# The last 64-row attention tile with full 128-column matmuls, and the engines' order planned anew

## The chip, the cores and the metric

The kernel runs on one core of a Trainium2 chip. The metric is the device time of one execution in microseconds (us), as the median of several runs. A profile is one execution recorded by the hardware profiler; its span goes from the first to the last instruction. TensorE is called PE in the rows, VectorE DVE, ScalarE ACT, GpSimd POOL and SyncE SP.

## What is computed

Three stages, each fed by the one before; inputs and output are float32, with 4 batches, 8 heads, 576 positions and a head size of 64.

```python
def _attn_ref(q, k, v):                       # q, k, v: (4, 8, 576, 64)
    scores = scale * np.matmul(q, k.transpose(0, 1, 3, 2))
    scores = np.where(block_i >= block_j, scores, -1e9)     # blocks of 64 positions
    attn = softmax(scores)
    return np.matmul(attn, v)

def _moe_ref(x, w_in, w_out):                 # x: (2304, 512), w_in: (512, 2048)
    h = x @ w_in
    return (h * np.tanh(softplus(h))) @ w_out

def _moe2_ref(x, w_gate, w_val, w_out, rms_g):   # (512, 1536) twice, (1536, 512)
    xn = x / rms(x) * rms_g
    g = xn @ w_gate
    return (silu(g) * (xn @ w_val)) @ w_out
```

## The kernel before

Most matrices are split into two float16 parts, high and low, and a product is made of three passes (`PASSES`: high-high, high-low, low-high). Batch 0's scores and the first four blocks of 64 rows are done in float32.

Attention goes through the 576 query rows of a batch in five tiles, four of 128 rows and a last one of 64 (`attention(b, i, ...)`, i = 0 to 4). `scores` makes the scores of one head (two heads in the first two tiles) in PSUM, DVE takes their maximum (L1003), `bias` is made of it on DVE or POOL (L1012), ACT takes the exponential (L1028). `probs` splits it into float16 parts (L1102 to L1109) and has a DMA transpose them (L1119). `av` multiplies the transposed probabilities `pt` (the weights) with the split values `v16` (the moving operand) into the PSUM buffer `xt` (L1146), of which there is one. `norm_x` multiplies by one over the sum (L1176, tile `xfl`), splits and transposes the result.

The last tile puts two heads on the 128 partitions, 64 rows each. Its four pairs of heads go through `av` as 2 heads x 5 key tiles x 3 passes; each matmul takes the 64 columns of its head from `pt` as weights and writes 64 partitions of `xt`. The fifth key tile has 64 rows only, so its matmuls use 64 rows.

The first MLP goes over nine tiles of 256 tokens: `mlp1_h` (L1366, float32 in the first tile: L1357) with the activation on ACT (L1392, L1385), a split on DVE, ACT or POOL (L1401 to L1409), then `mlp1_y` (L1427, first tile L1435) and the RMS norm. It runs beside attention, which feeds it. The second MLP (`mlp2_gv` L1778, `mlp2_o` L1913) follows. Weights come as 512 KB pieces and are brought to float32 by DVE operations between SBUF tiles (`to_f32`, L566, L574, L594), squared and summed for a scale (`group_scale`, tile `wc`, L641), and split (`split`, L516 to L539).

The order of every engine's instructions is computed before the kernel is built. Each operation is recorded with `op(engine, ns, fn, r=..., w=..., at=..., alts=...)`: a cost in ns, what it reads and writes, a wished time, and other engines that could do it. `Plan.place` is a list scheduler that plays the operations forward with these costs: at each step it takes the engine that is free first and the ready operation with the smallest key. `LAT` holds the delay from one engine's end to another's start. Costs come from `t_act`, `t_dve`, `t_dve2`, `t_dvett`, `t_pool`, `t_pool1` and `t_mm`. `t_dve2` and `t_dvett` are those of DVE operations between SBUF tiles; they are of the class `Shared`, and `place` makes them longer by a share while POOL is busy:

```python
if e == DVE and not back and type(ns) is Shared and free[POOL] > t:
    ns = ns + ns.by * min(free[POOL] - t, ns / (1.0 - ns.by))
```

`Plan.run` places several times, with keys from a backward pass, and keeps the shortest. `SHIFT` adds a number to the keys of each named part of the work. In waits of the first part of the plan `with_idle` puts matmuls on a constant (L1967).

## Time and profile before

| | us |
|---|---|
| median of 3 runs | 970.93 |
| lowest and highest run | 969.48, 971.12 |
| span of the profiled execution | 967.8 |

The profiled execution's time is known by its span alone; the runs are 1.7 to 3.3 us longer than that. In the rows, a busy column is the time in which an engine had an instruction running. The end of a matmul is modelled, so the pace of a run of matmuls is read from one start to the next start. `PEclk` is the clock granted to TensorE as a share of 2.4 GHz. Idle time stands in square brackets behind an instruction, with what ended it.

### The profile page before, as it was taken

What the parts mean: (1) busy time and instruction counts of PE and PEld (TensorE: products, weight loads), DVE (VectorE), ACT (ScalarE), POOL (GpSimd) and SP (SyncE); (2) the same over time, 40 slices, a digit from 0 to 9 for tenths busy, and PEclk for the clock granted to TensorE, in tenths of its full rate; (3) what the DMA queues carried; (4) which work ended last, traced back from release to release, by engine and by line L of the source; (5) the groups of instructions that cost most, each with busy time, mean ns of one, the idle gap of its engine ahead of it and who ended that gap; (6) DMA issues with size and microseconds to landing.
All of it is one profiled execution on the core that took longest, in us unless ns stands there. A gap on an engine that the chain in (4) does not pass through costs nothing.

```text
span 967.8 us, 19320 instructions
## 1 busy us (share of the span) xinstructions
PE 943.2 (97%) x6958; PEld 591.0 (61%) x6959; DVE 789.4 (82%) x1760; ACT 597.2 (62%) x1225; POOL 561.4 (58%) x709
## 2 busy tenths in 40 slices
PE   9997989999999999999999999999999999999998
PEld 7783447666585767675675845555555555554554
DVE  4898888888877879688875999989997898866745
ACT  4767578999768889875984555456543364531320
POOL 1268247878665746577752937858864487531411
PEclk9997999999999999999999999999999999999999
DMA  9765476779966896686763746781836260753011
GB/s 238 194 211 154 140 152 127 116 134 169 170 138 122 142 169 139 108 174 150 144 152 60 150 107 156 164 184 52 160 118 115 88 125 14 135 94 87 1 61 70
DMA packets 317183, 125.39 MB, mean 130 GB/s; under 512 B 296352, under 2 KB 296352, under 8 KB 317088
## 3 DMA queue, kind: packets, MB, share of 16 engines
q1 hardware_dynamic: 317088, 124.17, 60.5%
q8 instruction: 54, 0.88, 0.4%
q14 instruction: 41, 0.34, 0.1%
HBM read 50.07 MB, written 12.98 MB: 65 GB/s over the span
## 4 chain that ended last, share of the span: by engine, by line
PE 55%; DVE 6%; DMA 2%; ACT 2%; POOL 1%; issue 1%; DVEq 0%; ACTq 0%; POOLq 0%
PE o L1913 13%; PE v L1778 11%; PE g L1778 10%; PE y L1427 9%; PE h L1366 8%; PE x L1146 2%; DMA pt<-p 1%; PE s L968 1%; DVE w2fo L574 0%; DMA w2ro<-in_moe_w_out_dram 0%; DVE w2fo L566 0%; POOL sums_b L1528 0%; PE s L986 0%; DVE u3v L1806 0%; ACT e L1028 0%
## 5 line engine op out<-in xcount | busy, mean ns | idle before, releaser
L1366 PE MATMUL h<-x,w1i 128*128 128x256 f16 x1536 | 179.8, 274 | 0.0
L1427 PE MATMUL y<-w1o,g 128*128 128x512 f16 x768 | 177.1, 379 | 1.1 <-DVE g L1409 1.0
L1366 PEld LDWEIGHTS <-w1i 128*128 128x128 f16 x1536 | 147.3, 98 | 22.3 <-issue 0.4
L1778 PE MATMUL g<-xnT,w2g 128*128 128x384 f16 x756 | 131.0, 326 | 1.3 <-DVE u3v L1806 0.6
L1778 PE MATMUL v<-xnT,w2v 128*128 128x384 f16 x756 | 127.6, 326 | 0.5 <-DVE sl12g L1806 0.5
L1427 PEld LDWEIGHTS <-g 128*128 128x128 f16 x768 | 70.9, 98 | 78.7 <-DVE g L1409 3.1
L1778 PEld LDWEIGHTS <-w2g 128*128 128x128 f16 x756 | 73.9, 98 | 54.4 <-issue 3.6
L1778 PEld LDWEIGHTS <-w2v 128*128 128x128 f16 x756 | 73.9, 98 | 51.6 <-issue 0.9
L1003 DVE TENSOR_REDUCE mx<-s 128x1 f32<-128x512 f32 (+4 forms) x128 | 69.7, 558 | 27.9 <-PE s L969 26.6
L1028 ACT ACTIVATE e<-s,bias,cS 128x512 f32<-128x512 f32 (+3 forms) x120 | 72.6, 608 | 19.5 <-POOL bias L1012 10.3
L1109 POOL TENSOR_TENSOR p<-e,p 128x128 f16<-128x128 f32 (+4 forms) x66 | 61.9, 942 | 16.5 <-DVE p L1102 6.2
L1146 PEld LDWEIGHTS <-pt 128*128 128x128 f16 (+2 forms) x1368 | 55.0, 103 | 24.7 <-issue 8.6
L1146 PE MATMUL x<-v,pt 128*128 128x64 f16 (+2 forms) x1368 | 63.2, 196 | 4.3 <-DMA pt<-p 2.1
L1409 DVE SCALAR_TENSOR_TENSOR g<-f,ich,g 128x512 f16<-128x512 f32 x64 | 58.0, 910 | 5.9 <-ACT g L1404 2.9
L1392 ACT ACTIVATE f<-h,ch 128x512 f32<-128x512 f32 x64 | 43.6, 685 | 15.6 <-PE h L1366 12.2
L1028 ACT ACT_TABLE_LOAD x39 | 50.0, 1283 | 4.0 <-DVE bias L1012 3.4
L1392 ACT ACT_TABLE_LOAD x39 | 50.0, 1283 | 0.7
L506 POOL TENSOR_SCALAR p<-e 128x128 f16<-128x128 f32 (+2 forms) x53 | 26.7, 505 | 34.9 <-ACT e L1028 20.1
L1796 ACT ACTIVATE p5v<-v,ck 128x384 f32<-128x384 f32 x18 | 10.5, 581 | 46.5 <-PE v L1778 46.5
L1102 DVE CAST p<-e 128x128 f16<-128x128 f32 (+2 forms) x58 | 25.9, 449 | 14.8 <-ACT e L1028 7.1
L1109 DVE TENSOR_TENSOR p<-e,p 128x384 f16<-128x384 f32 (+4 forms) x46 | 33.7, 734 | 5.1 <-POOL p L506 3.9
L1012 POOL TENSOR_SCALAR bias<-mx,nS 128x1 f32<-128x1 f32 (+1 forms) x46 | 25.1, 545 | 21.5 <-DVE mx L1003 17.1
(610 smaller groups left out, 2190.1 us busy)
## 6 DMA issues: line engine op xcount, KB each, us to landing
wir<-in_moe_w_in_dram SPq DMA_DIRECT2D x16, 512.0 KB, 6.0
wor<-in_moe_w_out_dram SPq DMA_DIRECT2D x16, 512.0 KB, 3.8
w2rg<-in_moe_w_gate_dram SPq DMA_DIRECT2D x24, 256.0 KB, 3.2
w2rv<-in_moe_w_val_dram SPq DMA_DIRECT2D x24, 256.0 KB, 3.5
w2ro<-in_moe_w_out_dram SPq DMA_DIRECT2D x24, 256.0 KB, 3.1
q<-in_q_dram SPq DMA_DIRECT2D x16, 256.0 KB, 3.8
k<-in_k_dram SPq DMA_DIRECT2D x16, 256.0 KB, 4.6
v<-in_v_dram SPq DMA_DIRECT2D x15, 256.0 KB, 4.7
```

The source lines that it names most:

```text
L506: nc.gpsimd.tensor_scalar(out=out_, in0=in_, scalar1=by, scalar2=1.0, op0=ALU.mult, op1=ALU.mult)
L1003: lambda z=z, cols=cols: nc.vector.reduce_max(out=mx()[:, cols], in_=ts[z](), axis=AX.X),
L1028: lambda y=y, z=z, c0=c0, w=w, acc=acc, e=e, h=h: nc.scalar.activation(out=e()[:, c0 : c0 + w], in_=ts[z]()[:, y, :], func=AF.Exp, bias=bi ...
L1102: lambda z=z, ev=ev, t0=t0, t1=t1: nc.vector.tensor_copy(out=view(p16)[:, z, t0:t1, 0, :], in_=ev(t0, t1)),
L1109: lo = lambda eng, z=z, ev=ev: eng.tensor_tensor(out=view(p16)[:, z, :, 1, :], in0=ev(0, kt), in1=view(p16)[:, z, :, 0, :], op=ALU.subtract)
L1146: nc.tensor.matmul(o, pv(z)[:nr, t, ph, c0 : c0 + w], v16[b, t]()[:nr, vh, h * D : h * D + D], start=(t == 0 and y == 0), stop=(t == kt - ...
L1366: nc.tensor.matmul(ph()[:, g, :], w1i[fq]()[:, cc, wh, f * P : (f + 1) * P], x()[:, xh * NCC + cc, :], start=(z == 0), stop=(z == 3 * NCC ...
L1392: ACT, t_act(W, 1, True), lambda: nc.scalar.activation(out=e(), in_=phf(), func=AF.Mish, scale=cs()),
L1409: lambda: nc.vector.scalar_tensor_tensor(out=g16()[:, 1], in0=hv(), scalar=sc(), in1=g16()[:, 0], op0=ALU.mult, op1=ALU.subtract),
L1427: nc.tensor.matmul(yps[t, m](), g16()[:, gh, g, m * P : (m + 1) * P], w1o[f]()[:, wh, :], start=(f == 0 and z == 0), stop=(f == NF1 - 1 an ...
L1778: nc.tensor.matmul(b(), w()[:, wo, wh, cc, :], x()[:, (2 * xo + xh) * 2 + cc, :], start=(i == 0), stop=(i == 5),)
L1913: nc.tensor.matmul(y(), pp()[:, gh, m * P : (m + 1) * P], w2["o", fq]()[:, g, wh, :], start=(g == 0 and i == 0), stop=(g == FQ - 1 and i = ...
```

## The change

`av` of the last tile takes both heads of a pair at once: all 128 columns of `pt` as weights, and the 128 columns of both heads' values as the moving operand, over all 128 rows. The result is 128 x 128; the quarter of head 0's rows with head 0's values and the quarter of head 1's rows with head 1's values are the wanted ones. `xt` is twice as wide there, and `norm_x` reads the two quarters with one DVE instruction each. Since all 128 rows of the fifth key tile are used, the unused 64 rows of its `v16` tile are set to zero by POOL or DVE.

The planner's numbers change: all delays in `LAT`, the costs of all engines (DVE and POOL operations shorter, delays between engines mostly longer, DMA issue times shorter), and the cost of the bursts of `av`. `Shared` has no share any more; instead `place` holds a lock that `Shared` operations of DVE and all operations of POOL take in turn, and an engine may prefer an operation that doesn't need the lock. `SHIFT` is replaced, and `FINE` adds a number for each of some 700 single operations. So all queues are ordered anew.

```diff
 LAT = {
-    PE: {PE: 0, ACT: 45, DVE: 45, POOL: 45, DMA: 45, NONE: 0},
-    ACT: {PE: 145, ACT: 45, DVE: 45, POOL: 178, DMA: 45, NONE: 0},
-    DVE: {PE: 110, ACT: 100, DVE: 45, POOL: 104, DMA: 35, NONE: 0},
-    POOL: {PE: 110, ACT: 45, DVE: 45, POOL: 45, DMA: 35, NONE: 0},
-    DMA: {PE: 820, ACT: 780, DVE: 780, POOL: 820, DMA: 820, NONE: 0},
+    PE: {PE: 0, ACT: 200, DVE: 200, POOL: 240, DMA: 200, NONE: 0},
+    ACT: {PE: 153, ACT: 133, DVE: 133, POOL: 180, DMA: 127, NONE: 0},
+    DVE: {PE: 131, ACT: 112, DVE: 112, POOL: 160, DMA: 106, NONE: 0},
+    POOL: {PE: 87, ACT: 68, DVE: 68, POOL: 113, DMA: 62, NONE: 0},
+    DMA: {PE: 640, ACT: 660, DVE: 660, POOL: 700, DMA: 650, NONE: 0},
...
+HOLD = {DVE: 100.0, POOL: 90.0}
...
+def shares(e, ns):
+    return e == POOL or e == DVE and type(ns) is Shared
...
+                        elif kind and lock - HOLD[e] > f:
+                            t = lock - HOLD[e]
+                            pull = t - f
...
-            if e == DVE and not back and type(ns) is Shared and free[POOL] > t:
-                ns = ns + ns.by * min(free[POOL] - t, ns / (1.0 - ns.by))
             start[i], end[i] = t, t + ns
+            if not back and shares(e, ns):
+                lock = end[i] = max(t + ns, lock + ns - HOLD[e])
...
 def t_act(n, aps=0, psum=False, accum=False):
-    return (110 if psum else 140) + 0.8333 * n + 70 * aps + (120 if accum else 0)
+    return (51 if psum else 93) + 0.8333 * n + 95 * aps + (92 if accum else 0)
...
 def t_dve(n, aps=0):
-    return 125 + 1.0417 * n + 85 * aps
+    return 70 + 1.0417 * n + 40 * aps
...
 def t_dve2(n, aps=0):
-    return Shared(158 + 0.5208 * n + 61 * aps, 0.6)
+    return Shared(70 + 0.5208 * n + 62 * aps)
...
 def t_dvett(n, aps=0):
-    return Shared(160 + 1.0417 * n + 61 * aps, 0.45)
+    return Shared(75 + 1.0417 * n + 66 * aps)
...
 def t_pool(n):
-    return 390 + 1.85 * n
+    return 175 + 1.9 * n
...
             x = buf("at", [P, 2, DM], F16, f"v16_{b}_{tt}", "v16", 6)
+            if n < P:
+                pad = lambda eng, x=x, n=n: eng.memset(x()[n:].bitcast(U32), 0)
+                op(POOL, 500, lambda pad=pad: pad(nc.gpsimd), w=[(x, 2)], at=a, alts=[(DVE, 600, lambda pad=pad: pad(nc.vector))])
...
-                outs = (
-                    [(xt()[BLK * hh : BLK * hh + BLK, cols, :], 2 * key + hh, BLK * hh, BLK) for hh in range(2)]
-                    if last
-                    else [(xt()[:, cols, :], key, 0, P)]
-                )
-                for o, h, c0, w in outs:
-                    for t in range(kt):
-                        nr = rows(t)
-                        for y, (vh, ph) in enumerate(PASSES):
-                            nc.tensor.matmul(
-                                o, pv(z)[:nr, t, ph, c0 : c0 + w], v16[b, t]()[:nr, vh, h * D : h * D + D],
-                                start=(t == 0 and y == 0), stop=(t == kt - 1 and y == 2),
-                            )
+                w = 2 * D if last else D
+                for t in range(kt):
+                    for y, (vh, ph) in enumerate(PASSES):
+                        nc.tensor.matmul(
+                            xt()[:, cols, :], pv(z)[:, t, ph, :], v16[b, t]()[:, vh, key * w : key * w + w],
+                            start=(t == 0 and y == 0), stop=(t == kt - 1 and y == 2),
+                        )
...
             op(
-                PE, 34 * 3 * kt * (2 if last else 1), mm, r=[pt] + [v16[b, t] for t in range(kt)],
+                PE, (56 if last else 34.2) * 3 * kt, mm, r=[pt] + [v16[b, t] for t in range(kt)],
...
-            op(
-                DVE, t_dve(256),
-                lambda: nc.vector.tensor_tensor(
-                    out=xf(), in0=xt(), in1=r().unsqueeze(2).to_broadcast([P, NPAIR, D]), op=ALU.mult
-                ),
-                r=[xt, r], w=[xf], at=at,
-            )
+            for hh in range(2 if last else 1):
+                sl, cl = (slice(BLK * hh, BLK * hh + BLK), slice(D * hh, D * hh + D)) if last else (slice(0, P), slice(0, D))
+                op(
+                    DVE, t_dve(256, 1),
+                    lambda sl=sl, cl=cl: nc.vector.tensor_tensor(
+                        out=xf()[sl], in0=xt()[sl, :, cl], in1=r()[sl].unsqueeze(2).to_broadcast([sl.stop - sl.start, NPAIR, D]),
+                        op=ALU.mult,
+                    ),
+                    r=[xt, r], w=[(xf, hh)], at=at,
+                )
...
-                    xt = ps_x([P, NPAIR, D], f"x{b}_{i}_{cnt[0]}")
+                    xt = ps_x([P, NPAIR, 2 * D if last else D], f"x{b}_{i}_{cnt[0]}")
...
```

## Rows read from the trace of the kernel before

**Rows 1.** The page's first part: busy us, share of span, instructions of each engine.
```profile
PE 943.2 (97%) x6958; PEld 591.0 (61%) x6959; DVE 789.4 (82%) x1760; ACT 597.2 (62%) x1225; POOL 561.4 (58%) x709
```
**Rows 2.** Busy us by stretch: length, PE, PEld, DVE, ACT, POOL, clock, DMA, GB/s.
```profile
0.00:50.00 50.00, 47.66 (x415) 38.84 (x416) 33.57 (x88) 27.69 (x80) 10.71 (x28) 1.00 0.85 218
50.00:100.00 50.00, 44.19 (x202) 29.33 (x203) 46.33 (x78) 35.58 (x77) 35.79 (x31) 0.90 0.59 179
100.00:150.00 50.00, 46.36 (x323) 25.36 (x322) 41.45 (x124) 33.23 (x86) 20.86 (x38) 0.93 0.63 142
150.00:570.00 420.00, 412.92 (x3837) 283.93 (x3834) 345.55 (x884) 333.38 (x652) 280.48 (x398) 1.00 0.72 139
570.00:968.00 398.00, 392.09 (x2189) 213.55 (x2186) 322.46 (x590) 167.32 (x331) 213.59 (x214) 1.00 0.46 101
```
**Rows 3.** The same view, two stretches of a lower clock.
```profile
77.00:87.40 10.40, 6.93 (x10) 2.05 (x9) 10.40 (x20) 6.24 (x17) 7.11 (x8) 0.51 0.66 206
142.00:149.00 7.00, 6.50 (x53) 4.99 (x54) 5.82 (x24) 4.11 (x9) 4.64 (x5) 0.51 0.76 157
```
**Rows 4.** TensorE in order of time: start, us, line, tiles, form, count; three bursts.
```profile
142.25 2.22 PE L1146 MATMUL x<-v,pt 128*64 128x64 f16 x30 [0.41 <-DMA pt<-p]
144.40 0.19 PE L480 MATMUL shared<-sqv,ones_h 128*128 128x5 bf16 x1
...
152.05 1.47 PE L1146 MATMUL x<-v,pt 128*64 128x64 f16 x30
153.45 0.39 PE L1366 MATMUL h<-x,w1i 128*128 128x256 f16 x2
...
521.22 1.47 PE L1146 MATMUL x<-v,pt 128*64 128x64 f16 x30
522.63 0.28 PE L1625 MATMUL shared<-junk,ones_h 128*128 128x256 bf16 x1
```
**Rows 5.** TensorE in order of time: score matmuls, and a burst with 128-column weights.
```profile
157.39 0.22 PE L968 MATMUL s<-kT,qT 128*128 128x128 f16 x1
157.45 0.22 PE L968 MATMUL s<-kT,qS 128*128 128x128 f16 x1
157.51 0.19 PE L969 MATMUL s<-mask_col,mask_row 128*128 128x64 bf16 x1
...
188.38 0.51 PE L1146 MATMUL x<-v,pt 128*128 128x64 f16 x12
```
**Rows 6.** Lines L1176 and L1023: duration ns min/median/max; who waited (us, times).
```profile
L1176 DVE TENSOR_TENSOR xfl<-x,r x36: 403/415/426, 19.1 to 522.7; 128x256 f32<-128x256 f32 x36
...
  PE x L1146: 0.6, 1
...
L1023 POOL MEMSET e<- x16: 147/152/168, 133.3 to 497.4; 128x64 f32 x16
```
**Rows 7.** POOL in order of time.
```profile
68.35 6.03 POOL L527 TENSOR_TENSOR w1i<-wis,w1i 128x512 f16<-128x512 f32 x4
```
**Rows 8.** DVE in order of time, from 68 to 81 us.
```profile
68.58 1.64 DVE L574 SCALAR_TENSOR_TENSOR wos<-wor,wos 128x512 uint32<-128x512 uint32 x1
...
74.58 0.68 DVE L594 SCALAR_TENSOR_TENSOR wos<-wor,wos 128x512 uint32<-128x512 uint32 x1
75.18 1.09 DVE L574 SCALAR_TENSOR_TENSOR wos<-wor,wos 128x512 uint32<-128x512 uint32 x1
...
77.76 1.64 DVE L539 SCALAR_TENSOR_TENSOR v<-v,sv,v 64x512 f16<-64x512 f32 x1
...
80.68 0.67 DVE L641 TENSOR_REDUCE wc<-wiq 128x1 f32<-128x512 f32 x1
```
**Rows 9.** TensorE in order of time; in brackets its idle time before, and what ended it.
```profile
76.50 0.55 PE L1074 MATMUL tpp<-ident,e 128*128 128x128 f32 x3 [2.07 <-ACT g L1385]
...
81.41 2.08 PE L1435 MATMUL y<-wos,spares 128*128 128x512 f32 x2 [2.90 <-DVE wc L641]
84.06 0.17 PE L480 MATMUL shared<-sqk,ones_h 128*128 128x5 bf16 x1 [0.57 <-ACT junk L750]
```
**Rows 10.** TensorE's waits by line and releaser: total us, times, longest.
```profile
PE x L1146 <- DMA pt<-p: 2.1, 5, 0.8
```

More of the change, by code (lines that the diff above doesn't have):

```diff
@@ L166, in place @@
                     t, p, i, z = heapq.heappop(w)
-                    heapq.heappush(q.setdefault(ops[i].table if e == ACT else None, []), (p + 0.3 * z, i, z))
+                    kind = ops[i].table if e == ACT else shares(e, ops[i].alts[z][1])
+                    heapq.heappush(q.setdefault(kind, []), (p + 0.3 * z, i, z))
                 first = None
-                for tb, h in q.items():
+                for kind, h in q.items():
                     while h and start[h[0][1]] is not None:
@@ L172, in place @@
                     if h:
-                        pull = 0.0 if tb is None or tb == table or back else TABLE_PULL
-                        if first is None or h[0][0] + pull < first[0]:
-                            first = h[0][0] + pull, h
-                if first is not None:
-                    c = (f, e, first[1])
-                else:
-                    while w and start[w[0][2]] is not None:
-                        heapq.heappop(w)
-                    if not w:
-                        continue
-                    c = (w[0][0], e, None)
+                        pull, t = 0.0, f
+                        if back:
+                            pass
+                        elif e == ACT:
+                            pull = 0.0 if kind is None or kind == table else TABLE_PULL
+                        elif kind and lock - HOLD[e] > f:
+                            t = lock - HOLD[e]
+                            pull = t - f
+                        if first is None or h[0][0] + pull < first[0]:
+                            first = h[0][0] + pull, t, h
+                while w and start[w[0][2]] is not None:
+                    heapq.heappop(w)
+                if first is not None and (first[1] <= f or not w or first[1] <= w[0][0]):
+                    c = (first[1], e, first[2])
+                elif w:
+                    c = (w[0][0], e, None)
+                else:
+                    continue
                 if best is None or c[:2] < best[:2]:
@@ L188, in place @@
                 _, i, z = heapq.heappop(heap)
+            elif e in HOLD and not back:
+                free[e] = t
+                continue
             else:
@@ L426, in const_of @@
         b = keep(name, w, dtype, parts)
-        op(DVE, 100, lambda: nc.vector.memset(b(), value), w=[b], at=-1e6)
+        op(DVE, 70, lambda: nc.vector.memset(b(), value), w=[b], at=-1e6)
         return b
@@ L770, in prep_k @@
         sq = small("sqk", NTT, 2)
-        op(POOL, 40, lambda: nc.gpsimd.memset(sq(), 0.0), w=[sq], at=at)
+        op(POOL, 75, lambda: nc.gpsimd.memset(sq(), 0.0), w=[sq], at=at)
         ts = []
@@ L806, in prep_v @@
         ts = []
-        op(POOL, 40, lambda: nc.gpsimd.memset(sq(), 0.0), w=[sq], at=at)
+        op(POOL, 75, lambda: nc.gpsimd.memset(sq(), 0.0), w=[sq], at=at)
         for tt in range(NTT):
@@ L860, in prep_q @@
         if n < P:
-            op(POOL, 40, lambda: nc.gpsimd.memset(sq(), 0.0), w=[sq], at=at)
+            op(POOL, 75, lambda: nc.gpsimd.memset(sq(), 0.0), w=[sq], at=at)
         t = load(q, "q", b, tt, at)
@@ L1016, in scores @@
             op(
-                DVE, 200, lambda: bias_of(nc.vector), r=[(mx, 2 * h) for h in keys] + m_in,
+                DVE, Shared(125), lambda: bias_of(nc.vector), r=[(mx, 2 * h) for h in keys] + m_in,
                 w=[(bias, h) for h in keys], at=at,
-                alts=[(POOL, 600, lambda: bias_of(nc.gpsimd))],
+                alts=[(POOL, 210, lambda: bias_of(nc.gpsimd))],
             )
@@ L1747, in load_xn @@
                     ),
[L1748 removed]
+                    r=[(xn_key, (p, m, part))], w=[(a, (m, part))], at=at, issue=T_DGE_XN[part == 2],
                 )
```

47 lines of the change are left out of this document (23 added, 24 removed), and 186 rows, old and new, of tables (FINE, SHIFT).

## The prediction

> **What bounds the kernel now.** I read the engine part of the page first: TensorE is busy 943.2 of 967.8 us, DVE 82%, ACT 62%, POOL 58% [rows 1]. The next view is the table of stretches [rows 2]. TensorE's idle time, stretch length less its busy column, is 2.34 us in the first 50 us, 5.81 in the next 50, 3.64 in the third 50, 7.08 in the 420 us in which attention and the first MLP run together, and 5.91 in the 398 us of the second MLP. So from 150 us on TensorE is busy 805.0 of 818 us: it is the bound there, no other engine comes near it (DVE 345.55 of 420, ACT 333.38), and a microsecond of matmuls that is taken out there is worth about a microsecond. Before 150 us it is not the bound: it idles 11.8 of 150 us, DVE is busy 46.33 of the 50 us from 50 to 100, and the granted clock is 0.90 and 0.93 in the second and third 50 us. The last point is placed by two narrow stretches: from 77.0 to 87.4 us and from 142 to 149 us the clock is 0.51, the lower level of 1.2 GHz, and 1.00 (2.4 GHz) before, between and after [rows 3]. At half clock for 10.4 and 7.0 us TensorE did 5.1 and 3.4 us less work than it could have.
>
> **The change, part one: fewer, wider matmuls in the last query tile.** Each of the 4 batches ends with a tile of 64 query rows, in which two heads share the 128 partitions. Before, a pair of heads takes 2 heads x 5 key tiles x 3 passes = 30 matmuls of 64 columns with 64-column weights; after, 5 x 3 = 15 of 128 columns with 128-column weights, whose off-diagonal quarters are thrown away. There are 4 pairs in each batch, so 16 bursts. Price before: from the start of a burst to the start of TensorE's next instruction, 152.05 to 153.45 = 1.40 us, and 521.22 to 522.63 = 1.41 [rows 4]; 15 of the 16 are like this (these are the first and the last of them), and one in the half-clock stretch lasts from 142.25 to 144.40 = 2.15. Sum 15 x 1.40 + 2.15 = 23.2 us. Price after: no row has this matmul, but the score matmuls of the first query tile have its shape (128x128 weights, 128 columns, f16, other weights each time): 157.39, 157.45, 157.51 [rows 5], so 56 to 60 ns from one to the next. The weights don't set that pace: 12 matmuls of 64 columns with 128-column weights last 0.51 us, of which 0.19 is the length of a lone one [rows 5], so (0.51 - 0.19) / 11 = 29 ns each. 15 x 0.056 = 0.84 us a burst, 16 bursts 13.4 us, and 14.3 if the one in the half-clock stretch stays there at double the price. Saving 8.9 to 9.8 us; I take 9.0. All bursts lie behind 142 us, where TensorE is the bound, so I count all of it on the path.
>
> The Trainium skill speaks against this price: its page "TensorE: Matmul & The Clock Gate", section "Back-to-back issue gap", gives some 81 ns for each 128-column matmul in a stream where every matmul has a weight load of its own. By it the bursts would cost 240 x 0.081 = 19.4 us and the saving, an estimate from that page, would be 3.7 us. The rows just read show such a stream at 56 to 60 ns, so the trace disagrees with it.
>
> **Part one, what it adds.** The normalisation of the tile now reads two quarters of the PSUM bank, by two DVE instructions on 64 partitions in place of one on 128. The old one takes 403 to 426 ns [rows 6]; both new ones have 256 elements a partition still, and no row shows that fewer partitions are faster, so I count one more of 0.41 us a batch, 1.7 us in all. It lies on DVE beside other work. It reaches TensorE only where the next burst waits for the single PSUM buffer of this result; in the whole trace that wait is 0.6 us, once [rows 6]. Between 0 and 1.7 us, I take 0.4. A memset of 64 rows x 512 words is added in each batch; the nearest rows are the memset of 64 columns at 152 ns [rows 6] and, from above, a 512-column subtraction of POOL beside a busy DVE, four in 6.03 us, 1.51 us each [rows 7]. It only has to be done before the tile's values are used, tens of microseconds later, on an engine busy 280 of 420 us: nothing on the path, up to 1.5 us a batch, 6 us in all, if the cover were gone.
>
> **Part two: the order.** No instruction apart from these is added or removed, but the planner that lays out every queue (TensorE, ACT, DVE, POOL, SP with its DMAs) is given other costs, other wishes, and a rule that a DVE operation between SBUF tiles and a POOL operation take turns. So every queue may be permuted, work with alternatives may change engine, and the table switches of ACT may become more or fewer. The trace tells two things on whether the new costs are nearer the chip. First, spacing: a DVE operation of 512 columns starts at 74.58 and the next at 75.18 [rows 8], 0.60 us; the new cost is 75 + 533 = 608 ns, the old one 160 + 533 = 693. Second, turns: in the same stretch the same operation takes 0.68 us once and 1.64 us another time [rows 8], while POOL does the four subtractions just priced. Five of the DVE operations between 68.58 and 79.4 us take 1.64 (those at 68.58 and 77.76 are the first and the last), 0.96 us too long each, 4.8 us together. The old planner made DVE slower by a share and POOL not at all.
>
> What this costs is seen on TensorE: it waits 2.07 us for ACT and then 2.90 us for the reduction "wc" of DVE [rows 9], which starts at 80.68 [rows 8], behind those five in DVE's queue. Then follows the stretch at half clock. If the new order spares DVE the 4.8 us in front of that reduction, the wait of 2.90 goes, the 0.57 us behind it go, and so do the 5.1 us of the first half-clock stretch, because TensorE then doesn't idle ahead of it: 8.6 us. What is late next is DVE itself (93% busy there), so I don't count more in this place. I count nothing of the second half-clock stretch and its 3.64 us of idle, and nothing of the 7.08 us in the long stretch: the new order will have waits of its own. A gain before 150 us reaches the end only because TensorE stays 98% busy behind it and DVE, ACT and DMA (0.72) have room.
>
> **Sum.** The profiled execution's span is 967.8 us; the median of the timed runs is 970.9, so 3.1 us lie around the span, which I leave as they are. 970.9 - 9.0 + 0.4 - 8.6 = 953.7 us.
>
> **Rivals.**
> (a) The order is a wash: what it mends at 70 to 90 us comes back as waits elsewhere. Then only part one counts: 970.9 - 8.6 = 962.3 us. For it: the present order loses only 7.08 of 420 us in the long stretch, and a permuted one can easily lose that again. Against it: the place where DVE and POOL block each other is plain.
> (b) The wide matmuls are bound by their weight loads. With the 29 ns of a load shown for 64 columns not overlapped with the 56 ns of the columns, a matmul costs 85 ns, a burst 1.28 us, and the saving is 23.2 - 20.4 = 2.8 us: 968.1 us with an order that is a wash. The page of the skill named above would put it there too. The rows at 56 to 60 ns are against it.
> (c) Slower: the new order lets TensorE run dry in places where it doesn't today. The mechanism is one gap of the kind at 74 to 82 us: 2.07 + 2.90 us of idle and the half-clock stretch behind it, 5.1 us, together 10.1 us. One such gap more, with the present two kept, turns 962.3 into 972.4; that is the point from which the kernel is slower, and a second makes 982. The likeliest place is between 50 and 150 us, where DVE is at 93% and every shift of it is seen at once, or where the attention of the next batch begins. Speaking for it: both half-clock stretches today came from just this. Against it: two such gaps would have to be made where the new costs fit the spacing better than the old.
> (d) Part one does not do what it says, because the bursts stand in time in which TensorE would wait anyway for the transposed probabilities. All waits of that kind are 2.1 us, five times [rows 10], among these 16 bursts and all those of the full tiles; so it could hide a quarter of the saving at most, unless the new order makes attention the bound. Then about 970 us, no change.
>
> **How the numbers follow.** Forecast 0.57 (its own range 944 to 960), (a) 0.20, (b) 0.05, (c) 0.10, (d) 0.05, and 0.03 that far more is recovered: both half-clock stretches, all of the idle time before 150 us and half of that in the long stretch, 9.0 + 8.5 + 11.8 + 3.5 = 33 us, so about 938. The range from 938 to 968.5 leaves out (c), (d) and what is below: under 2 in 10. A measurement of this kernel can tell about 0.2%, 1.9 us. Faster by more than that: 0.57 + 0.20 + 0.05 + 0.03 = 0.85; within: 0.05; slower: 0.10.
>
> **What would show it.** In the changed kernel the 128-column matmuls of these tiles should number 240 and each burst last about 0.84 us. Right for part two: no reduction of DVE that TensorE waits for near 80 us, the DVE operations of 512 columns there near 0.68 us, and a clock of 1.00 from 50 to 100 us. Wrong: the clock row still shows about 0.51 for 10 us or in a new place; TensorE's idle time from 150 to 570 us above 10 us; bursts of 1.2 us or more; or waits of TensorE for the normalisation of more than 2 us in all.

## The result and the profile after

The changed kernel takes 959.11 us, the median of four runs (957.22 to 960.48), against 971.02 for the kernel before: a ratio of 0.9885 with an interval of 0.9865 to 0.9904. That is 11.9 us less, where 17.2 were forecast (953.7). The time lies in the range. The profiled execution has a span of 956.5 us.

The page's first part of the changed kernel, as [rows 1]: TensorE's busy time is 11.0 us less, POOL's 51.5 us.

```profile
PE 932.2 (97%) x6754; PEld 585.3 (61%) x6755; DVE 785.3 (82%) x1797; ACT 600.5 (63%) x1244; POOL 509.9 (53%) x659
```

Busy time by stretch, as [rows 2] and with the same columns:

```profile
0.00:50.00 50.00, 46.87 (x435) 38.38 (x436) 34.57 (x97) 30.97 (x89) 8.50 (x25) 1.00 0.87 222
50.00:100.00 50.00, 49.77 (x267) 34.81 (x267) 48.11 (x96) 37.56 (x81) 34.16 (x32) 1.00 0.52 167
100.00:150.00 50.00, 47.51 (x372) 29.24 (x371) 41.33 (x111) 36.64 (x90) 14.47 (x29) 1.00 0.80 170
150.00:570.00 420.00, 405.80 (x3557) 274.84 (x3555) 350.80 (x918) 333.94 (x664) 251.66 (x372) 1.00 0.73 140
570.00:957.00 387.00, 382.22 (x2132) 208.04 (x2130) 310.46 (x580) 161.41 (x323) 201.15 (x202) 1.00 0.46 100
```

TensorE's idle time is 0.23 us from 50 to 100 us (5.81 before) and 5.85 us in the first 150 us (11.8 before). The clock is 1.00 in each row: both stretches at half clock are gone. From 150 to 570 us, however, the idle time has doubled, from 7.08 to 14.2 us.

Where the time was won is read from the first float16 matmul of the first MLP, in order of time on TensorE. The first line is of the kernel before:

```profile
144.87 1.02 PE L1366 MATMUL h<-x,w1i 128*128 128x256 f16 x4
```

and this one of the changed kernel:

```profile
134.25 0.50 PE L1378 MATMUL h<-x,w1i 128*128 128x256 f16 x3
```

So the changed kernel is 10.6 us ahead at 134 us, and the spans differ by 11.3 us at the end. All that follows, 15 of the 16 wide bursts among it, added 0.7 us to that lead.

The lead is a real one: worked out from the two traces, TensorE has done the same work up to this point (114.2 and 113.6 us of matmuls at full clock, matmuls on the constant left out). In the kernel before it idled 11.8 us until then and was busy at half clock for 9.1 us, so that 4.6 us of work were lost, some of it where a wait would have come instead (see the filled gaps below); in the changed kernel it idled 4.1 us and lost nothing to the clock. The changed kernel spends 2.3 us more on matmuls on the constant.

The reason for the early lead stands in DVE's queue (in order of time: start, duration, engine, line, tiles, form), as [rows 8]:

```profile
70.22 0.69 DVE L586 SCALAR_TENSOR_TENSOR wos<-wor,wos 128x512 uint32<-128x512 uint32 x1
73.40 0.69 DVE L653 TENSOR_REDUCE wc<-wiq 128x1 f32<-128x512 f32 x1 [0.53 <-PE wiq L622]
74.53 1.53 DVE L586 SCALAR_TENSOR_TENSOR wos<-wor,wos 128x512 uint32<-128x512 uint32 x1
```

and on TensorE in the same place, as [rows 9]:

```profile
75.36 1.89 PE L1369 MATMUL h<-x,wis 128*128 128x256 f32 x8
77.09 0.49 PE L1089 MATMUL tpp<-ident,e 128*128 128x128 f32 x3
78.68 0.55 PE L1089 MATMUL tpp<-ident,e 128*128 128x128 f32 x3
79.07 3.60 PE L1447 MATMUL y<-wos,spares 128*128 128x512 f32 x8
```

The last reduction "wc" is at 73.40 and no longer at 80.68, and now DVE waits for TensorE there, 0.53 us, and not the other way round. The operation of 512 columns at 70.22 lasts 0.69 us; the slow kind, 1.53, comes behind the reduction. TensorE goes from h to y without a wait.

The wide bursts, on TensorE in order of time:

```profile
154.71 1.00 PE L1155 MATMUL x<-v,pt 128*128 128x128 f16 x15
155.55 0.82 PE L1378 MATMUL h<-x,w1i 128*128 128x256 f16 x6
...
512.70 1.00 PE L1155 MATMUL x<-v,pt 128*128 128x128 f16 x15
513.53 1.24 PE L1439 MATMUL y<-w1o,g 128*128 128x512 f16 x5
```

A burst of 15 takes 0.84 us to the next start, 56 ns a matmul, against 1.40 [rows 4]. For 16 bursts that is 9.0 us less work. Counted from each start to TensorE's next instruction they take 15.3 us, against 23.15, because waits of the changed kernel lie between a burst and the next instruction.

Why the old burst takes 1.40 us is seen from one start to the next in it: 31 to 32 ns between matmuls of the same form, but 122 to 126 ns wherever the form changes, from 128 rows of weights to the 64 of the fifth key tile, back, and to the next instruction's full array. There are four such changes in a burst, some 0.37 us above the pace of 32 ns. By this reckoning most of the 0.56 us saved belongs to these changes and not to the width; a kernel with narrow matmuls over all 128 rows, which would part the two, was not run.

TensorE's waits from 150 to 570 us (total us, times, longest) have grown:

```profile
PE s L983 <- ACT e L1043: 4.2, 9, 0.9
PE x L1155 <- DMA pt<-p: 3.2, 6, 0.9
PE y L1439 <- DVE w1o L551: 1.7, 3, 0.9
```

Of the 16 bursts 15 lie behind the first float16 matmul. From there to the end TensorE is busy 8.1 us less than before and idle 7.4 us more. How much of these waits comes from the bursts and how much from the new order is parted below.

What the change added, by source line: the normalisation (L1187) and the memset (L838), each with durations in ns, minimum, median, maximum.

```profile
L1187 DVE TENSOR_TENSOR xfl<-x,r x40: 394/416/429, 18.8 to 514.2; 128x256 f32<-128x256 f32 x32, 64x256 f32<-64x256 f32 x8
  PE x L1155: 0.4, 2
L838 POOL MEMSET v<- x3: 520/521/687, 157.5 to 397.4; 64x512 uint32 x3
L838 DVE MEMSET v<- x1: 485/485/485, 0.9 to 0.9; 64x512 uint32 x1
```

The second line says that TensorE waited for the normalisation twice, 0.4 us in all (0.6 us, once, before [rows 6]). Nobody waited for the memsets.

### The profile page after: what moved, and what is told of

Same layout as the page of the kernel before. It is cut to its first block, busy times and chain, and to the rows that moved or that the text cites. A ratio compares the mean times of both kernels' runs of the same rounds, so it can differ in the third digit from the quotient of the medians.

```text
span 956.5 us, 18899 instructions
## 1 busy us (share of the span) xinstructions
PE 932.2 (97%) x6754; PEld 585.3 (61%) x6755; DVE 785.3 (82%) x1797; ACT 600.5 (63%) x1244; POOL 509.9 (53%) x659
## 5 line engine op out<-in xcount | busy, mean ns | idle before, releaser
L1790 PE MATMUL g<-xnT,w2g 128*128 128x384 f16 x756 | 129.0, 326 | 0.0
L1790 PEld LDWEIGHTS <-w2g 128*128 128x128 f16 x756 | 73.8, 98 | 51.5 <-issue 0.4
L1043 ACT ACTIVATE e<-s,bias,cS 128x512 f32<-128x512 f32 (+4 forms) x120 | 72.5, 607 | 21.0 <-POOL bias L1027 11.0
L1421 DVE SCALAR_TENSOR_TENSOR g<-f,ich,g 128x512 f16<-128x512 f32 x64 | 55.4, 871 | 10.7 <-ACT g L1416 6.6
L1155 PEld LDWEIGHTS <-pt 128*128 128x128 f16 x1128 | 48.7, 98 | 22.2 <-DMA pt<-p 8.2
L1155 PE MATMUL x<-v,pt 128*128 128x64 f16 (+1 forms) x1128 | 55.5, 199 | 4.2 <-DMA pt<-p 3.4
L1124 POOL TENSOR_TENSOR p<-e,p 128x512 f16<-128x512 f32 (+4 forms) x54 | 50.4, 937 | 6.5 <-DVE p L1117 2.9
L1828 POOL TENSOR_TENSOR p5g<-u2g,p5g 128x384 f32<-128x384 f32 x15 | 15.9, 1058 | 58.3 <-DVE sl22g L1828 54.6
L1124 DVE TENSOR_TENSOR p<-e,p 128x384 f16<-128x384 f32 (+4 forms) x58 | 37.6, 650 | 8.4 <-ACT p L1120 4.9
L983 PE MATMUL s<-kT,qT 128*128 128x384 f16 (+3 forms) x96 | 27.5, 299 | 6.1 <-ACT e L1043 5.9
```

The lines of the kernel that those rows point to most:

```text
L983: nc.tensor.matmul(t, src[b, i]()[:, h, :], kT[b]()[:, h, 0:n], start=(ph == 0), stop=False)
L1043: lambda y=y, z=z, c0=c0, w=w, acc=acc, e=e, h=h: nc.scalar.activation(out=e()[:, c0 : c0 + w], in_=ts[z]()[:, y, :], func=AF.Exp, bias=bi ...
L1124: lo = lambda eng, z=z, ev=ev: eng.tensor_tensor(out=view(p16)[:, z, :, 1, :], in0=ev(0, kt), in1=view(p16)[:, z, :, 0, :], op=ALU.subtract)
L1155: nc.tensor.matmul(xt()[:, cols, :], pv(z)[:, t, ph, :], v16[b, t]()[:, vh, key * w : key * w + w], start=(t == 0 and y == 0), stop=(t == ...
L1421: lambda: nc.vector.scalar_tensor_tensor(out=g16()[:, 1], in0=hv(), scalar=sc(), in1=g16()[:, 0], op0=ALU.mult, op1=ALU.subtract),
L1790: nc.tensor.matmul(b(), w()[:, wo, wh, cc, :], x()[:, (2 * xo + xh) * 2 + cc, :], start=(i == 0), stop=(i == 5),)
```

## The experiments

Two theories stood at the start. The first is the prediction's: TensorE is the bound behind 150 us, so shorter bursts count in full, and before 150 us the collision of DVE and POOL costs a wait and a stretch at half clock. The rivals: the shorter bursts only uncover other waits, and the half clock costs nothing because something else is late there.

### Each half of the change alone

The wide matmuls in the order before:

```diff
-                                o, pv(z)[:nr, t, ph, c0 : c0 + w], v16[b, t]()[:nr, vh, h * D : h * D + D],
+                w = 2 * D if last else D
...
+                            xt()[:, cols, :], pv(z)[:, t, ph, :], v16[b, t]()[:, vh, key * w : key * w + w],
```

> The order of before, untouched on every queue, with the 128-column matmuls of the last tile (and the memset and the second normalising instruction that they need) put into it. Theory T (TensorE is the bound where the 16 bursts lie, so their saving is on the path): 971.0 - 9.0 + 0.4 = 962.4 us, bursts of 0.84 us in place of 1.40, both half-clock stretches of before still there. Rival H (the bursts stand in time in which TensorE would wait anyway): 969 to 971 us, with TensorE's idle time from 150 to 570 us up from 7.1 to about 14 us.

The 64-column matmuls in the new order:

```diff
-                w = 2 * D if last else D
...
-                            xt()[:, cols, :], pv(z)[:, t, ph, :], v16[b, t]()[:, vh, key * w : key * w + w],
+                                o, pv(z)[:nr, t, ph, c0 : c0 + w], v16[b, t]()[:nr, vh, h * D : h * D + D],
```

> The order of the changed kernel, untouched on every queue, with the 64-column matmuls of before put back into it (the rows of zeros and the two normalising instructions stay). Theory T (the bursts are on the path in either order): 959.1 + 8 to 9 = 967 to 968 us. Rival W (in the new order the attention chain, not TensorE, is what ends last between 150 and 570 us, so the wide matmuls buy nothing there; TensorE idles 14.2 us in that stretch, 7.1 before): 959 to 963 us, with the idle time of that stretch down to 6 to 10 us.

| median us (ratio to before, interval) | order before | new order |
|---|---|---|
| 64 columns | 970.72 | 964.33 (0.9919 to 0.9943) |
| 128 columns | 966.42 (0.9937 to 0.9961) | 959.11 (0.9865 to 0.9904) |

The wide matmuls save 4.3 us in the one order and 5.2 in the other, not 9; the order saves 6.4 and 7.3. The two parts add up to within 0.9 us. The profile of the first kernel has only one of the two half-clock stretches, 79.4 to 89.6 us, against what was expected; but its first float16 matmul comes at 145.68, no earlier than the 144.87 of before, so the 4.3 us are not owed to that. The long stretch of the first and then of the second kernel, columns as above:

```profile
150.00:570.00 420.00, 407.70 (x3621) 279.50 (x3619) 351.85 (x902) 331.99 (x652) 279.50 (x401) 1.00 0.73 139
```

```profile
150.00:570.00 420.00, 407.71 (x3746) 277.08 (x3745) 340.89 (x909) 332.44 (x659) 250.86 (x370) 1.00 0.73 139
```

Idle time there is 12.3 us in each, 5.2 more than before. So the new order by itself loses 5.2 us in that stretch, and the wide matmuls by themselves lose as much: in the old order the waits for the transposed probabilities grew from 1.7 to 3.1 us. Both together lose 7.1 us (14.2), so on top of the new order the wide matmuls add 1.9 us.

### The half-clock stretches filled

111 matmuls on a constant were put into the waits of the kernel before, at 74, 77 to 81 and 138 to 140 us, so that TensorE is kept running.

```diff
+            for _ in range(EXTRA.get(o.idx, 0)):
+                self.idle()
...
+EXTRA = {548: 30, -1: 45, 754: 36}
```

> The kernel before with 111 matmuls on a constant put into three waits of TensorE at 74, 77 to 81 and 138 to 140 us (30, 45 and 36 of them, some 56 ns each, so inside those waits at full clock); nothing else is moved. Theory C (the half clock behind those waits costs real time): both stretches at 0.51 go, and the time falls by the work lost at half clock behind the waits, (87.4 - 81.4) / 2 = 3.0 and (149 - 142.25) / 2 = 3.4 us, to about 964.6 us. Rival D (DVE and the attention chain bind there, so a faster TensorE only waits more): 969 to 971 us, with the idle time between 80 and 150 us up by as much as the clock gave.

The kernel became slower, 973.34 us, ratio 1.0026 (1.0015 to 1.0037). Two stretches and two lines of TensorE in order of time:

```profile
75.50:82.80 7.30, 5.05 (x53) 3.57 (x53) 7.30 (x8) 4.46 (x12) 7.24 (x5) 1.00 0.79 212
82.80:89.60 6.80, 5.71 (x16) 2.64 (x16) 6.06 (x17) 5.18 (x12) 3.38 (x5) 0.50 0.61 181
138.00:150.00 12.00, 9.60 (x132) 7.33 (x132) 9.41 (x42) 7.79 (x21) 6.83 (x10) 1.00 0.87 150
```

```profile
80.82 1.13 PE L1440 MATMUL y<-wos,spares 128*128 128x512 f32 x2 [0.97 <-DVE wc L643]
83.89 0.17 PE L482 MATMUL shared<-sqk,ones_h 128*128 128x5 bf16 x1 [1.95 <-ACT junk L752]
```

The clock stays at 1.00 until 82.8 us and from 138 to 150 us, the second half-clock stretch is gone, and the first float16 matmul of the first MLP comes 1.95 us later than before. Until 83.9 us the rival is right: with the clock up TensorE only waits longer for ACT's `junk`, 1.95 us in place of 0.57, and is 0.17 us ahead there.

The first half-clock stretch was not removed, however, but moved: it lasts from 82.8 to 89.6 us here and from 77.2 to 87.4 before. Behind `junk`, until 90 us, TensorE waits for nothing in either kernel, and what it then does shows the price of the clock. The kernel before, then this one:

```profile
87.79 1.96 PE L1435 MATMUL y<-wos,spares 128*128 128x512 f32 x4
89.59 0.43 PE L1146 MATMUL x<-v,pt 128*128 128x64 f16 x9
```

```profile
87.97 2.78 PE L1440 MATMUL y<-wos,spares 128*128 128x512 f32 x4
90.59 0.42 PE L1148 MATMUL x<-v,pt 128*128 128x64 f16 x9
```

The same four matmuls take 1.80 us to the next start at full clock and 2.62 mostly at half. At 90.6 us the kernel is 1.00 us late, for a half clock that lasts 2.2 us longer, and it is still 0.99 us late at 135 us. So half clock costs nothing before `junk` arrives and its full price behind it. The other 0.96 us of the delay arise between 141.6 and 146.8 us, where the full clock of the second stretch went into waits. What a kernel without the half clock behind `junk` would take was not measured.

### POOL's part in the collision taken away

In the kernel before, POOL's 16 subtractions for the low half of `w_in` became memsets of zeros.

```diff
+            plan_part = plan.part
...
-                POOL, t_pool(n), lambda: nc.gpsimd.tensor_tensor(out=lo(), in0=src(), in1=hi(), op=ALU.subtract),
+                POOL, t_pool(n), lambda: nc.gpsimd.memset(lo(), 0.0) if plan_part.startswith("wis") else nc.gpsimd.tensor_tensor(out=lo(), in0=src(), in1=hi(), op=ALU.subtract),
```

> The kernel before with POOL's 16 subtractions for the low halves of the first MLP's input weights left out; a memset of zeros stands in their places, so these halves are zero. Theory P (the step of the prediction: POOL beside DVE makes five DVE operations 4.8 us longer in front of the reduction that TensorE waits for at 81 us): those five take 0.68 us, the wait of 2.90 us shrinks to under 0.5, the half-clock stretch at 77 us goes or shrinks, and the time falls by 5 to 8.6 us to 962 to 966 us. Rival Q (DVE is full there in any case, or the wait of 2.07 us for ACT alone brings the half clock): the reduction starts 3 us or more earlier but the half-clock stretch stays and the time falls by less than 3 us, to 968 or above.

966.80 us against 970.72, ratio 0.9954 (0.9940 to 0.9969): 3.9 us less, between the two expectations. DVE's reduction and two lines of TensorE:

```profile
74.28 0.67 DVE L642 TENSOR_REDUCE wc<-wiq 128x1 f32<-128x512 f32 x1
```

```profile
75.33 0.55 PE L1075 MATMUL tpp<-ident,e 128*128 128x128 f32 x3 [1.68 <-ACT g L1386]
80.70 0.17 PE L480 MATMUL shared<-sqk,ones_h 128*128 128x5 bf16 x1 [3.11 <-ACT junk L751]
```

The five operations that took 1.64 us [rows 8] take 0.67 to 0.73, and "wc" comes 6.4 us earlier, as the collision theory says. That DVE and POOL hold each other up is also what the Trainium skill states ("SBUF — State Buffer", section "Terms": the two share a pair of ports, and the one that loses it is blocked for the other's whole instruction). The trace agrees so far, with 1.64 against 0.68 us beside subtractions of 1.51; what DVE does in the time between no row shows. TensorE's wait of 2.90 us for "wc" makes room for one of 3.11 us for ACT's `junk`, so TensorE still waits in this place. But `junk` is earlier too: TensorE is past it at 80.70 us and no longer at 84.06, 3.4 us ahead. Of these 2.3 us are left at the first float16 matmul (142.59); half clock, which sets in during the wait of 3.11 us (79.7 to 86.5 us), had cost 1.2 us by 87.4 us.

The same edit in the changed kernel:

> The changed kernel with POOL's 16 subtractions for the low half of w_in (512 columns each) replaced by memsets of zeros, so that the low half of w_in is left out; in the order before the same edit saved 4.2 us. Theory T (the new order has taken the collision of DVE and POOL off the path, which is what its gain before 150 us consists of): the time changes by less than 1.5 us, 957.5 to 960. Rival U (the collision is still there and the gain came from work that changed engine, three of POOL's scalings to ACT): it falls by 3 to 5 us, to 954 to 956.

959.03 us (956.74 to 961.58), no change against 959.11, and the first float16 matmul comes at 133.60 in place of 134.25. In the new order the collision is off the path, and ACT's wait too (the lines at 75.36 to 79.07 above).

### What uncovers the waits of the long stretch: ACT's table loads?

ACT loads a table 76 times in that stretch, 97.6 us in all. In the kernel before, and with the wide matmuls in addition, the Mish of the first MLP became a plain copy, which needs no table (the same was done in the first tile's line).

```diff
-            ACT, t_act(W, 1, True), lambda: nc.scalar.activation(out=e(), in_=phf(), func=AF.Mish, scale=cs()),
+            ACT, t_act(W, 1, True), lambda: nc.scalar.activation(out=e(), in_=phf(), func=AF.Copy, scale=cs()),
```

> The kernel before with the activation of the first MLP replaced by a plain copy on ACT, of the same shape and with the same scale (the result is another function of h). The copy needs no table of its own, so ACT's switches between two tables, 76 of 1.283 us in the stretch from 150 to 570 us (97.6 of 420 us), should disappear; nothing else changes in any queue. It is the base for the next kernel. Theory A (in the long stretch the chain of attention, scores to ACT's exponential to the transposing DMA, is nearly as long as TensorE's work, and ACT is what makes it so): TensorE's idle time there, 7.08 us, falls to 2 to 4 us, total 965 to 968. Rival B (the chain is held by DVE, POOL or the DMA, not by ACT): idle stays 6 to 7 us, total 969 to 971.

> The same as e5_no_table_loads, with the wide AV matmuls of the changed kernel in addition. Beside e5 it measures what the wide matmuls save when ACT has 98 us more room. Theory A: the saving rises from the 4.3 us that it is with table loads to 7.5 to 9 us, near the 7.9 us by which the bursts themselves are shorter. Rival B: it stays at 4 to 5.5 us.

The first gave 969.92 us, ratio 0.9998 (0.9983 to 1.0013), the second 963.60, ratio 0.9928 (0.9910 to 0.9945). The long stretch of the first:

```profile
150.00:570.00 420.00, 411.85 (x3828) 283.13 (x3827) 344.07 (x886) 234.20 (x575) 283.67 (x399) 1.00 0.75 139
```

ACT is 99 us less busy, and TensorE idles 8.15 us, not less than the 7.08 before. Theory A falls for the narrow matmuls. The wide ones save 6.3 us here in place of 4.3, between the two expectations, and with these intervals 6.3 and 4.3 can't be told apart for certain. So the same was done in the new order:

> The changed kernel with the activation of the first MLP replaced by a plain copy of the same shape (the result is another function of h), so that ACT loses its 72 table loads, 92.4 us, in the long stretch. In the order before this brought nothing with narrow matmuls (ratio 0.9998) and let the wide ones save 6.3 us in place of 4.3. Theory A2 (the wide matmuls have brought TensorE to the point where the chain of attention holds it, and ACT is a part of that chain): TensorE's idle time from 150 to 570 us falls from 14.2 to 9 to 11 us, total 954 to 957. Rival F (the waits come from an order of instructions that is fixed for other lengths, and from DVE, POOL and the transposing DMA; ACT plays no part): idle 13 to 15 us, total 958 to 961.

961.06 us (959.93 to 961.90), idle time 19.1 us:

```profile
150.00:570.00 420.00, 400.94 (x3531) 271.95 (x3529) 344.29 (x910) 242.16 (x589) 255.13 (x371) 1.00 0.74 140
```

Both expectations missed the idle time, but ACT's table loads are not what holds TensorE in the new order.

### Still shorter bursts

The changed kernel with one of the three passes in the last tile's bursts:

```diff
-                    for y, (vh, ph) in enumerate(PASSES):
+                    for y, (vh, ph) in enumerate(PASSES[:1] if last else PASSES):
...
-                            start=(t == 0 and y == 0), stop=(t == kt - 1 and y == 2),
+                            start=(t == 0 and y == 0), stop=(t == kt - 1 and y == (0 if last else 2)),
```

> The changed kernel with only the first of the three passes in the bursts of the 64-row tiles: 5 matmuls in place of 15, 80 in place of 240, so about 9 us more of TensorE's work is gone (160 x 0.056 us); the high-low and low-high products of those rows are left out. If TensorE alone bounds the long stretch, the time falls by 8 to 9.5 us, to 950. If the chain of attention has become the bound there (the 7.9 us of shorter bursts already brought only 4 to 5), it falls by 2 to 5 us, to 954 to 957, and TensorE's idle time from 150 to 570 us grows from 14.2 to 18 to 21 us.

It is slower than the changed kernel, 963.49 us (961.50 to 963.71). One stretch at a lower clock, the long stretch, and two groups of TensorE's waits in it:

```profile
115.00:119.00 4.00, 4.00 (x24) 2.81 (x25) 3.25 (x7) 3.03 (x9) 1.21 (x3) 0.66 0.08 15
150.00:570.00 420.00, 397.08 (x3416) 266.00 (x3416) 344.67 (x914) 335.55 (x666) 252.23 (x372) 1.00 0.73 140
```

```profile
PE s L983 <- ACT e L1043: 9.0, 14, 2.3
PE x L1155 <- DMA pt<-p: 8.2, 11, 1.9
```

Some 9 us of TensorE's work are gone, and its idle time in the long stretch is 22.9 us, 8.7 more. The first float16 matmul is also 4.1 us late here, 3.5 of them from a wait for ACT and the lower clock behind it (TensorE in order of time):

```profile
114.89 1.12 PE L978 MATMUL s<-kT,qT 64*128 64x512 f32 x2 [0.88 <-ACT e L1043]
```

So the question was put again with the first batch left as it is:

```diff
-                    for y, (vh, ph) in enumerate(PASSES[:1] if last else PASSES):
+                    for y, (vh, ph) in enumerate(PASSES[:1] if last and b else PASSES):
...
```

> The changed kernel with 5 matmuls in place of 15 in the 12 bursts of batches 1 to 3 alone (two of the three passes left out there), about 6.7 us less work for TensorE (120 x 0.056 us), all behind 250 us; everything before is the changed kernel's. It repeats the question of e7_thin_av without that run's late start, where a wait of 0.88 us at 114.9 and a stretch at half clock cost 4.1 us before the first thinned burst. If TensorE alone bounds the long stretch: 952 to 953.5. If the chain behind the waits holds it: 956.5 to 960, with 4 to 7 us more idle time of TensorE from 150 to 570 us than the 14.2 of the changed kernel.

963.30 us, and with a wide spread (959.10 to 968.30). The long stretch and its two largest waits:

```profile
150.00:570.00 420.00, 397.74 (x3421) 266.60 (x3419) 343.47 (x910) 332.25 (x661) 249.32 (x370) 1.00 0.73 139
```

```profile
PE x L1155 <- DMA pt<-p: 8.5, 11, 3.1
PE s L983 <- ACT e L1043: 5.8, 9, 1.4
```

Idle time 22.3 us, 8.1 more than in the changed kernel, for 6.7 us of work taken out. No microsecond of it reached the end.

The median is even 4.2 us above the changed kernel's, and the profiled span 4.3 us (960.8 against 956.5), more than either theory says. The trace shows where. The first burst with fewer passes starts at 255.27, where the changed kernel had its burst at 253.77: 1.5 us were lost ahead of any edited matmul. Then comes the longest wait, and behind it a clock of 0.50 from 269.8 to 273.2 us, which the row above rounds away. TensorE in order of time, and the same place in the changed kernel:

```profile
269.29 0.45 PE L1155 MATMUL x<-v,pt 128*128 128x128 f16 x5 [3.07 <-DMA pt<-p]
269.58 4.44 PE L1439 MATMUL y<-w1o,g 128*128 128x512 f16 x12
```

```profile
267.30 2.75 PE L1439 MATMUL y<-w1o,g 128*128 128x512 f16 x12
```

To the next start the 12 matmuls take 4.28 us here and 2.59 there: 1.7 us by the clock. At 274 us the kernel is 4.0 us behind, and at the end 4.3, though eight of the shortened bursts, 4.5 us of work, lie between: this is the clearest sign that shorter bursts bring nothing more. The long wait needs no shortened burst, either: the profile of the changed kernel without POOL's subtractions has one of 2.60 us for the same DMA in the same place, ahead of a burst of 15, with half clock behind it (268.6 to 272.0), and the changed kernel one of 0.91. So this place differs between executions, and a difference of some 3 us between two single profiles can come from it alone.

Is it the order, which was laid out for longer bursts? The planner was told the shorter cost:

```diff
-                PE, (56 if last else 34.2) * 3 * kt, mm, r=[pt] + [v16[b, t] for t in range(kt)],
+                PE, (56 * kt if last else 34.2 * 3 * kt), mm, r=[pt] + [v16[b, t] for t in range(kt)],
```

> e7_thin_av (5 matmuls in all 16 bursts, two passes left out) with the planner told so (the cost of a burst is 5 x 56 ns in place of 15 x 56), so that every queue is laid out anew for the shorter bursts. If the saving of shorter bursts is lost because a fixed order was laid out for longer ones, it comes back here: idle time from 150 to 570 us at 14 us or less in place of 22.9, total 948 to 953. If the chain of attention itself is too long, the idle time stays above 18 us and the total at 957 to 964.

966.55 us (964.35 to 970.55), idle time 28.0 us:

```profile
150.00:570.00 420.00, 392.03 (x3364) 263.55 (x3363) 345.18 (x884) 342.59 (x660) 267.58 (x381) 1.00 0.72 136
```

An order laid out anew doesn't bring the saving back. Its profile has a half-clock stretch as well, 423.9 to 427.3 us. It permutes every queue, though, and the numbers added to its keys (`SHIFT`, `FINE`) were not made for it, so this speaks against the rival without closing it.

### The transposed probabilities unhooked

> e10_thin_late (5 matmuls in the 12 last-tile bursts of batches 1 to 3) in which all AV matmuls of batches 1 to 3 take a constant tile of zeros as weights in place of the transposed probabilities. The transposing DMAs, the splits and every queue stay, but TensorE no longer waits for them; those rows of the result are left out. e10_thin_late had 22.3 us of idle time of TensorE from 150 to 570 us, 8.5 of them in waits for the transposed probabilities, at a span of 960.8 us. Theory G (the transposed probabilities, the last link of the chain of attention, are what holds TensorE): the 8.5 us go, idle time 13 to 15 us, span 951 to 954. Rival H (the links before it hold TensorE as well: scores wait for buffers that ACT's exponentials release): the waits move there, the waits of scores for ACT's exponential grow from 7.4 us to 11 or more, idle time 18 to 22 us, span 957 to 961.

```diff
-                            xt()[:, cols, :], pv(z)[:, t, ph, :], v16[b, t]()[:, vh, key * w : key * w + w],
+                            xt()[:, cols, :], idle_in().bitcast(F16) if b else pv(z)[:, t, ph, :], v16[b, t]()[:, vh, key * w : key * w + w],
```

956.92 us (956.65 to 961.34), 6.4 less than the kernel that it is made from, the one with fewer passes in batches 1 to 3; span 955.1, between the two expectations.

```profile
150.00:570.00 420.00, 401.49 (x3445) 270.23 (x3443) 349.09 (x920) 334.48 (x665) 254.31 (x374) 1.00 0.72 140
```

```profile
PE s L983 <- ACT e L1043: 7.1, 10, 1.4
PE y L1439 <- DVE sums_b L1493: 2.8, 1, 2.8
```

The waits of 8.5 us for the transposed probabilities are gone, but the idle time falls only by 3.8, to 18.5 us. The waits of scores for ACT's exponential, in both source lines together, grew from 7.4 to 8.4 us, not to the 11 that rival H asks for, so neither theory holds as it was written. One place shows what happens. With the probabilities TensorE waited 3.07 us at 269.29 (above); unhooked, the same place:

```profile
267.37 2.90 PE L1439 MATMUL y<-w1o,g 128*128 128x512 f16 x9 [2.82 <-DVE sums_b L1493]
```

The wait of 3.07 for the DMA covered one of 2.82 for DVE, and half clock follows this one too (268.6 to 272.0 us). By these two profiles, somewhat more than half of the waits for the transposed probabilities, 4.7 of 8.5 us, come back as waits for DVE, ACT and other DMAs.

## Why the prediction was right, and where it was not

**The direction and the range hold**, and the sum is 5.3 us too large: 8.6 us net were forecast for part one, 4.3 to 5.2 measured; 8.6 for part two, 6.4 to 7.3 measured. The range was 30 us wide. The time lies 5.4 us from the forecast and 3.2 us from the 962.3 of rival (a), whose mechanism, that what the order mends comes back as waits elsewhere, came in part.

**The step that failed: "a microsecond of matmuls that is taken out there is worth about a microsecond".** It was read from TensorE's busy share, 412.92 of 420 us [rows 2]. The 9.0 us by which the bursts became shorter, a term that was forecast rightly, were worth 4.3 and 5.2, and another 6.7 to 9 us of them were worth nothing. The busy share says that TensorE has little idle time now; it doesn't say how much room the next chain has. That room was about 5 us: behind it TensorE waits for the exponentials of ACT and the transposing DMAs, 0.9 us at the longest in the changed kernel and 1.4 to 3.1 us in those with fewer passes in its order. Rival (d) was this mechanism. I bounded it by today's waits for the transposed probabilities, 2.1 us [rows 10], but a wait shows what is already late, not what will be late next. It is shown that shorter bursts turn into waits (the two halves alone, and both kernels with fewer passes), that ACT's table loads are not the reason, and that the probabilities are somewhat less than half of it. Half clock behind the longest waits adds to the loss in the kernels with fewer passes, 1.7 us in the one profile where it was counted. Which of the other links would have to be shortened first stays open.

**The price of the wide burst was right.** 0.84 us a burst were forecast from the score matmuls [rows 5], and 0.84 measured, with 240 matmuls at 56 ns. Rival (b) is out. The Trainium skill's figure of some 81 ns ("TensorE: Matmul & The Clock Gate", section "Back-to-back issue gap") would have made it 1.2 us, an estimate from that page. The trace does not agree with it. What the prediction did not see is why the old burst was dear: the changes between 128 and 64 rows, 122 to 126 ns each.

**Normalisation and memset cost nothing on the path.** The waits for the normalisation are 0.4 us where they were 0.6 before, so the 0.4 us that were added for it did not come. The memset takes 485 to 687 ns, within its bounds, and nobody waits for it.

**The order: its size nearly, its working only in part.** The collision of DVE and POOL was the right place: "wc" comes 7.3 us earlier, and the wait of 2.90 and both half-clock stretches are gone. But of the 8.6 us, 5.1 were put on the clock, because TensorE would not idle ahead of it once "wc" came early. The stretch begins at 77.2 us, ahead of the wait for "wc" (78.5 to 81.4) and behind the wait of 2.07 us for ACT, so it could not hang on "wc" alone. The filled gaps show that half clock costs nothing until ACT's `junk` arrives at 84.06 and its full price from there to 87.4: about 1.7 of the 5.1 us. And the wait of 2.90 doesn't go by sparing DVE alone; the next one, for ACT, was 3.11 us. "What is late next is DVE itself" was wrong: ACT was. The lead of 10.6 us at the first float16 matmul is less idle time and no half clock, worked out above; how much of it is owed to DVE, POOL and ACT each was not measured. The new order then gives 5.2 us back in the long stretch (12.3 against 7.08 us of idle time with the old matmuls), which the prediction named as a sign of being wrong ("above 10 us") and did not count. Two errors of opposite sign, the lead and what is given back, left the term nearly right, which is luck.

**Rival (c), the slower side,** didn't come in the changed kernel, but its mechanism exists: in the kernel with one pass, a wait of 0.88 us at 114.89 and the lower clock behind it cost 3.5 us, and in the one with fewer passes in batches 1 to 3 half clock behind the wait of 3.07 us cost 1.7 us.

## What to carry to other kernels

Before counting work taken off a 98% busy engine as time won, ask how late its inputs come: with every queue laid out to arrive just in time, the first 9 us of shorter matmuls were worth 5, and the next 7 nothing. A wait that is removed is not won in full: look for what ends second in the same place (ACT's 3.11 behind DVE's 2.90, DVE's 2.82 behind the DMA's 3.07), and take the gain from the time at which TensorE is past the place (3.4 us in the first case), not from the waits. A stretch at half clock costs something only where TensorE is what is late; one such stretch can have a part that costs nothing and a part that costs its full price. A mean clock of 1.00 over a long stretch can hide one, so look at it in narrow windows.

## What the runs showed of the hardware

- With other weights each time, 128x128 weights and 128 columns follow each other at 56 ns over 240 matmuls, at a granted clock of 1.00. In the kernel before, 30 matmuls of 64 columns on half the array's columns took 1.40 us [rows 4], 47 ns each in the mean: a quarter of the products in 0.84 of the time.
- That mean hides two prices. From start to start these matmuls follow each other at 31 to 32 ns where the form stays the same (52 to 53 right behind a change), and 122 to 126 ns where it changes between 128 and 64 rows of weights (46 such changes from 149 us on).
- A wait of 0.88 us of TensorE (at 114.89) was followed by a mean clock of 0.66 from 115 to 119 us, one of 3.07 us (at 269.29) by 0.50 from 269.8 to 273.2. In another kernel, matmuls on a constant in the waits kept the clock at 1.00 until 82.8 us, but half clock set in during the next wait (1.95 us, until 83.9), and the kernel was 0.26% slower.
- A DVE operation of 512 columns between SBUF tiles takes 0.67 to 0.73 us alone and 1.64 beside POOL's subtraction; removing POOL's side moved DVE's queue by 6.4 us.
